# A down-projection weight loaded in another layout: twelve rows per partition and a rest of 256 rows over six or eight load engines

## The chip, the cores and the metric

The kernel runs on one core of one Trainium2 chip. The metric is the device time of one execution in microseconds (us). The time before is 231.94 us, the median of three runs (231.25 to 231.98). The core has TensorE (PE for matmuls, PEld for its weight loads), VectorE (DVE), ScalarE (ACT), GpSimd (POOL) and SyncE (SP), which here issues nearly all DMAs. A DMA is carried out by up to 16 DMA engines; they are called load engines here, to keep them apart from the compute engines. Each of them works through its own queue of packets, and when its part of a DMA is done it raises that DMA's semaphore.

## The reference, cut to what matters

One decode step for two sequences. The output is the sum of the input, a sliding-window attention and a gated unit, both fed by the same layer norm:

```python
xn = layernorm(A_x)                                  # (2, 1, 512)
# attention: 32 heads of 128 over 8 kv heads, the last 4096 of 32768 cached positions
q  = xn @ wq                                         # wq 512 x 4096
p  = softmax(q . k * 128**-0.5);  o = p . v          # k, v: 2 x 8 x 4096 x 128 read
# gated unit
h  = relu_gate(xn @ W_gate) * (xn @ W_up)            # W_gate, W_up 512 x 1792
out = x + o @ wo + h @ W_down                        # wo 4096 x 512, W_down 1792 x 512
```

All of it is float32. Keys and values of the window are 32 MB each, wq and wo 8 MB each, the three weights of the gated unit 3.5 MB each: some 95 MB, every byte read once.

## The kernel before, in words

**Loads.** Every large tile lies in a ring of four buffers (`ring`, `RING = 4`, L17 and L60) of up to 32 KB per partition. SP issues the loads in this order: two halves of wq, W_gate, W_up, then keys and values in tiles of 4 MB in turn (`load_kv`, L108), then `load_down` (L92, called at L445), then wo in two tiles, the first in one piece, the second in four pieces of 8, 5, 2 and 1 rows per partition (L475 to L480). A load into the ring waits until the tile that had the buffer has been used. All these loads stand in the load engines' queues in the order in which SP issues them. An ordinary load covers all 128 partitions, and each of 16 load engines gets eight of them.

**The rest of W_down before.** W_down has 1792 rows of 2 KB. `load_down` cuts them into 32 runs of 56 rows. Of each run 48 rows go into the main DMA (L98: 12 rows for each of 128 partitions, 24 KB in one piece), and 8 rows are left over, as four pieces of two rows (4 KB). The left-over pieces, 256 rows or 512 KB, are loaded by five DMAs at L105: three that take 8 runs each (32 partitions, 128 KB) and two that take 4 runs each (16 partitions, 64 KB). The first four go into spare columns of the ring buffer; the last goes into the tile `wx` of its own (L90). A memset (L99) on POOL clears the partitions of a spare column that no DMA fills.

**The gated unit.** Matmuls at L240 make the gate and the up product, `g_ps` and `u_ps`. The 1792 columns are cut into four quarters of 448, one for each group of 32 partitions of the result; the four matmuls of a step work on different column groups of PE. ACT copies the gate (L245), DVE makes the relu (L247) and the product `hh` (L251, L255). Matmuls against the identity (L263, L268) turn `hh` so that the 1792 values lie along partitions as the rows of W_down do, and DVE copies them to `hT` (L273, L275). This is done while the first keys arrive. The down product itself (L469 to L473) is made near the end.

**Attention.** For each group of heads, keys are transposed on PE (L296, result `pk`), copied to `kT` in a pool of two buffers (`ktp`, L61) by DVE and ACT in turn (L285), multiplied with q (L309, result `s`), put through a softmax (L315 on) and multiplied with the values (L373, result `o`). The order of all instructions is written out by hand.

**The end.** After the last values come the down product (`project` with `dw` and `wx`), the spreading of the last heads (L403) and the product with wo (L460, result `y_ps`), row by row of the wo tiles as their pieces land. One DVE copy (L482) and one DMA (L483) bring the result out.

Of the kernel before, what the change touches and what calls it, by code (L numbers as in the profile page):

```python
# [9 lines left out]
F32 = mybir.dt.float32  # L10
AF = mybir.ActivationFunctionType
ALU = mybir.AluOpType
# [8 lines left out]
def kernel(  # L21
# [12 lines left out]
    nc = tc.nc  # L34
    P = 128
    B, _, D = x.shape
# [3 lines left out]
    F = w_gate.shape[1]  # L40
    W = min(4096, max(256, SK // 4))
    KC = D // P
# [3 lines left out]
    Q = 4  # L46
# [6 lines left out]
    PK = P // 2  # L53
    J = W // PK
    FB = F // P
    FQ = F // Q
# [22 lines left out]
    def load_ff(w, name):  # L79
        return load(name, w.rearrange("(p k) f -> p k f", p=P), [P, KC, F])  # L80
# [3 lines left out]

    FR = F // 32
    FM = FB - 2
    assert FR == 4 * FM + 8
    wx = const.tile([16, 2, D], F32, name="wx")  # L90

    def load_down():  # L92
        t = ring.tile([P, FM + 4, D], F32, name="wd", tag="ring")
        runs = w_down.rearrange("(i x) e -> i x e", i=32)
        main = bass.AP(
            tensor=w_down.tensor, offset=w_down.offset, ap=[[FR * D, 32], [FM * D, 4], [1, FM * D]]
        )
        nc.sync.dma_start(t[:, 0:FM].rearrange("p k e -> p (k e)"), main)  # L98
        nc.gpsimd.memset(t[32:64, FM + 2:], 0.0)  # L99
        for i, n, dst in (  # L100
            (0, 8, t[0:32, FM:FM + 2]), (8, 8, t[32:64, FM:FM + 2]), (16, 8, t[0:32, FM + 2:]),
            (24, 4, t[32:48, FM + 2:]), (28, 4, wx),
        ):
            src = runs[i:i + n, 4 * FM:, :].rearrange("i (y s) e -> i y (s e)", s=2)
            nc.sync.dma_start(dst.rearrange("p s e -> p (s e)"), src)  # L105
# [25 lines left out]
    ident = const.tile([P, P], F32, name="ident")  # L131
# [7 lines left out]
    eps_t = const.tile([32, 1], F32, name="eps_t")  # L139
    nc.vector.memset(eps_t, EPS)  # L140

    hT = const.tile([P, FM + 6, B, 16], F32, name="hT")
# [66 lines left out]
    for kc in range(KC):  # L209
        for r in range(R):  # L210
            for c in range(C):
                n = r * C + c
                nc.tensor.matmul(  # L213
                    q_ps[r][32 * c:32 * c + 32, :], xnT[:, 0, kc, :], wqt[kc // 2][:, kc % 2, n * 512:(n + 1) * 512],
                    start=(kc == 0), stop=(kc == KC - 1),
                )
    gw = load_ff(w_gate, "wg")
    uw = load_ff(w_up, "wu")
    for r in range(R):
        qs = work.tile([P, 512], F32, name=f"qs{r}", tag="qs")  # L220
# [6 lines left out]
        for b in range(B):  # L227
            dst = qz[:, r * B + b].rearrange("p (a s h k) -> p a s h k", a=NP, s=S1, h=2)
# [3 lines left out]
                )  # L232


    g_ps = ps_kt.tile([P, FQ], F32, name="g_ps", tag="kt")
    u_ps = ps_kt.tile([P, FQ], F32, name="u_ps", tag="kt")
    for dst, wt in ((g_ps, gw), (u_ps, uw)):
        for kc in range(KC):
            for c in range(Q):
                nc.tensor.matmul(  # L240
                    dst[32 * c:32 * c + 32, :], xnT[:, 1, kc, :], wt[:, kc, c * FQ:(c + 1) * FQ],
                    start=(kc == 0), stop=(kc == KC - 1),
                )
    gs = work.tile([P, FQ], F32, name="gs", tag="qs")
    nc.scalar.copy(gs, g_ps)  # L245
    gr = work.tile([P, FQ], F32, name="gr", tag="qs")
    nc.vector.scalar_tensor_tensor(gr, gs, 0.0, gs, op0=ALU.is_gt, op1=ALU.mult)  # L247
    hh = work.tile([P, FB, 32], F32, name="hh", tag="qs")
    gv = gr.rearrange("p (i x) -> p i x", i=8)
    uv = u_ps.rearrange("p (i x) -> p i x", i=8)  # L250
    nc.vector.tensor_tensor(  # L251
        hh[:, 0:FM].rearrange("p k (i y) -> p i y k", i=8), gv[:, :, 0:4 * FM].rearrange("p i (y k) -> p i y k", y=4),
        uv[:, :, 0:4 * FM].rearrange("p i (y k) -> p i y k", y=4), op=ALU.mult,
    )
    nc.vector.tensor_tensor(  # L255
        hh[:, FM:].rearrange("p s (i y) -> p i y s", i=8),
        gv[:, :, 4 * FM:].rearrange("p i (y s) -> p i y s", s=2),
        uv[:, :, 4 * FM:].rearrange("p i (y s) -> p i y s", s=2), op=ALU.mult,
    )
    ht_ps = ps_1.tile([P, FM + 6, B], F32, name="ht_ps", tag="misc")  # L260
    for k in range(FM):
        for c in range(Q):
            nc.tensor.matmul(  # L263
                ht_ps[32 * c:32 * c + 32, k], hh[:, k], ident[:, 32 * c:32 * c + B], start=True, stop=True
            )
    for s in range(2):
        for c, p0, k, cols in ((0, 0, 0, (0, 32)), (1, 32, 0, (0, 32)), (2, 0, 2, (0, 32)), (3, 32, 2, (0, 16)), (3, 0, 4, (16, 32))):
            nc.tensor.matmul(  # L268
                ht_ps[p0:p0 + cols[1] - cols[0], FM + k + s], hh[:, FM + s, cols[0]:cols[1]],
                ident[:, 32 * c:32 * c + B], start=True, stop=True,  # L270
            )
    for n, lo, hi in ((P, 0, FM), (64, FM, FM + 2)):
        nc.vector.tensor_copy(hT[0:n, lo:hi, :, 0], ht_ps[0:n, lo:hi])  # L273
    for p0, n, lo, hi in ((0, 32, FM + 2, FM + 4), (32, 16, FM + 2, FM + 4), (0, 16, FM + 4, FM + 6)):
        nc.vector.tensor_copy(hT[p0:p0 + n, lo:hi, :, 0], ht_ps[p0:p0 + n, lo:hi])  # L275

# [117 lines left out]
    def finish(g):  # L394
        r, b = divmod(g, B)
        if b == 0:
            osb[r] = const.tile([HR, B, P], F32, name=f"osb{r}")
        nc.vector.tensor_scalar(osb[r][:, b], oa[g], rls[g], 2.0, op0=ALU.mult, op1=ALU.mult)

    def spread_heads(r):  # L400
        op = ps_1.tile([P, NJ, B], F32, name=f"op{r}", tag="misc")
        for e in range(NE):
            nc.tensor.matmul(  # L403
                op, spread[:, e].rearrange("h k e -> h (k e)"),
                osb[r][:, :, e * NJ:(e + 1) * NJ].rearrange("h b j -> h j b"),
                start=(e == 0), stop=(e == NE - 1),
            )
        nc.vector.tensor_copy(oT[:, r, :, :, 0], op)
# [33 lines left out]
    g = NG - 1  # L442
    scores(*pend.pop())
    vin = [load_kv(v_cache, "v", g, a) for a in range(NP)]
    dw = load_down()  # L445
    for _ in softmax(g):
        pass

# [9 lines left out]
    def project(lhsT, w, stop):  # L458
        for e in range(Q):
            nc.tensor.matmul(  # L460
                y_ps[32 * e:32 * e + 17, :], lhsT.rearrange("p b s -> p (b s)")[:, 0:17],
                w[:, e * P:(e + 1) * P], start=False, stop=stop,
            )
# [2 lines left out]
        values(g, a, vin[a])  # L466
        gather(g, a)
    finish(g)
    for k in range(FM + 4):  # L469
        n = P if k < FM else 64  # L470
        project(hT[0:n, k], dw[0:n, k], False)
    for k in range(2):
        project(hT[0:16, FM + 4 + k], wx[:, k], False)  # L473
# [38 lines left out]
```

## Time and profile before

| | |
|---|---|
| time, median of three runs | 231.94 us (231.25 to 231.98) |
| span of the profiled execution, first to last instruction | 230.3 us |
| PE busy | 184.4 us (80%) |
| DVE, ACT busy | 67.1 us, 48.4 us |
| bytes moved, mean rate | 95.15 MB, 413 GB/s |
| mean granted clock of TensorE | 0.933 |

The profile gives the span of its one execution and not that execution's time by the clock that timed the runs; the span is 1.6 us below the median. The page's first part is busy time by engine; a busy PE is not a PE at its peak, because matmuls are pipelined. Its second part cuts the span into 40 slices. "DMA" there, and "DMA share" in the windows, is the time that packets took as a share of 16 load engines; a packet is counted in the window in which it starts. The views do not keep the 16 load engines apart. The trace's semaphore records have the time at which each load engine finished its part of a DMA, without saying which engine it was.

### The profile page before, as it was taken

The numbers are of one execution on the slowest core, as the hardware profiler recorded it, in microseconds if no ns is written. First come the engines' busy times: TensorE is split into PE (matmuls) and PEld (weight loads), VectorE is DVE, ScalarE is ACT, GpSimd is POOL, SyncE is SP. The second block draws the span as 40 slices with busy tenths as digits, with TensorE's granted clock in tenths as the row PEclk, the third lists the DMA queues.
The fourth block names the chain that finished last, engine by engine and source line by source line (L and its number), as shares of the span: only waits on it lengthen the run. The fifth ranks groups of instructions, "written<-read, shape, count | busy, mean of one in ns | idle before, by whom it ended". The sixth has DMA issues, their size and how long they took to land.

```text
span 230.3 us, 4141 instructions
## 1 busy us (share of the span) xinstructions
PE 184.4 (80%) x1872; PEld 112.3 (49%) x1872; DVE 67.1 (29%) x136; ACT 48.4 (21%) x81; POOL 6.6 (3%) x23
## 2 busy tenths in 40 slices
PE   0295960849999889998999799589999974979593
PEld 0251220239666573664584565338566522148482
DVE  0500021023544462441472341147234123010000
ACT  2000100003444461540252331025133102000000
POOL 8100000000000000000000000000000100000000
PEclk9999799575999999999999999979999997699889
DMA  7999999999999999999999999999999999999980
GB/s 274 450 433 411 443 423 455 410 427 447 438 407 433 448 427 404 441 438 427 413 450 425 433 421 435 433 433 427 430 438 430 415 438 421 423 451 404 422 328 21
DMA packets 3936, 95.15 MB, mean 413 GB/s; under 512 B 454, under 2 KB 462, under 8 KB 848
## 3 DMA queue, kind: packets, MB, share of 16 engines
q1 hardware_dynamic: 3916, 94.90, 96.3%
q8 instruction: 14, 0.23, 0.4%
q14 instruction: 2, 0.02, 0.0%
q10 hardware_dynamic: 4, 0.00, 0.0%
HBM read 94.90 MB, written 0.00 MB: 412 GB/s over the span
## 4 chain that ended last, share of the span: by engine, by line
PE 46%; DMA 44%; DVE 4%; POOL 2%; ACT 1%; issue 1%; POOLq 0%
DMA k<-in_A_k_cache_dram 25%; PE pk L296 23%; DMA wd<-in_B_W_down_dram 11%; PE s L309 9%; DMA wo<-in_A_wo_dram 8%; PE o L373 5%; PE q_ps L213 3%; PE xt_ps L203 2%; PE pp L353 1%; DVE kT L285 1%; ACT p L342 1%; PE y_ps L460 1%; PE op L403 1%; PE oa L389 1%; POOL spread L155 1%
## 5 line engine op out<-in xcount | busy, mean ns | idle before, releaser
L296 PE MATMUL pk<-ident,k 128*128 128x128 f32 x512 | 68.1, 287 | 4.9 <-DMA k<-in_A_k_cache_dram 4.9
L296 PEld LDWEIGHTS pk<-ident,k 128*128 128x128 f32 x512 | 57.9, 146 | 19.8 <-issue 15.6
L285 DVE COPY kT<-pk 128x512 f32<-128x512 f32 x64 | 44.2, 691 | 50.6 <-PE pk L296 40.6
L285 ACT COPY kT<-pk 128x512 f32<-128x512 f32 x64 | 37.5, 586 | 81.8 <-PE pk L296 81.8
L309 PE MATMUL s<-kT,qz 128*32 128x512 f32 x256 | 31.9, 615 | 0.0
L373 PE MATMUL o<-v,pt 128*32 128x512 f32 x256 | 31.9, 631 | 0.0
L373 PEld LDWEIGHTS o<-v,pt 128*32 128x32 f32 x256 | 11.2, 116 | 15.3 <-issue 10.6
L309 PEld LDWEIGHTS s<-kT,qz 128*32 128x32 f32 x256 | 7.2, 112 | 12.8 <-issue 12.4
L213 PE MATMUL q_ps<-wq,xnT 128*32 128x512 f32 x64 | 10.9, 844 | 3.1 <-DMA wq<-in_A_wq_dram 2.6
L460 PE MATMUL y_ps<-wo,oT 128*17 128x128 f32 x256 | 9.3, 308 | 3.6 <-DMA wo<-in_A_wo_dram 3.6
L203 PE MATMUL xt_ps<-rep,xn 2*128 2x32 f32 x16 | 3.7, 400 | 10.2 <-DVE xn L197 10.2
L389 PE MATMUL oa<-on,pick 128*16 128x128 f32 x64 | 8.3, 273 | 4.1 <-DVE on L285 3.3
L285 DVE COPY on<-o 128x512 f32<-128x512 f32 x4 | 2.8, 692 | 29.9 <-PE o L373 29.9
L389 PEld LDWEIGHTS oa<-on,pick 128*16 128x16 f32 x64 | 5.8, 97 | 11.1 <-DVE on L285 7.0
L240 PE MATMUL u_ps<-wu,xnT 128*32 128x448 f32 x32 | 5.6, 870 | 6.8 <-DMA wu<-in_B_W_up_dram 6.8
L460 PEld LDWEIGHTS y_ps<-wo,oT 128*17 128x17 f32 x256 | 7.6, 111 | 5.1 <-DMA wo<-in_A_wo_dram 4.5
L203 PEld LDWEIGHTS xt_ps<-rep,xn 2*128 2x128 f32 x16 | 3.6, 319 | 10.2 <-issue 10.2
L285 ACT COPY on<-o 128x512 f32<-128x512 f32 x4 | 2.3, 586 | 26.6 <-PE o L373 26.6
L213 PEld LDWEIGHTS q_ps<-wq,xnT 128*32 128x32 f32 x64 | 2.5, 150 | 10.8 <-issue 6.6
L353 PE MATMUL pp<-ident,p 128*128 128x128 f32 x32 | 5.2, 295 | 2.4 <-ACT p L342 1.5
L342 ACT ACTIVATE p<-s,nm 128x1024 f32<-128x1024 f32 x4 | 4.5, 1116 | 12.5 <-DVE nm L337 12.5
L240 PEld LDWEIGHTS u_ps<-wu,xnT 128*32 128x32 f32 x32 | 1.4, 168 | 10.9 <-DMA wu<-in_B_W_up_dram 7.6
(77 smaller groups left out, 67.6 us busy)
## 6 DMA issues: line engine op xcount, KB each, us to landing
k<-in_A_k_cache_dram SPq DMA_DIRECT2D x8, 4096.0 KB, 26.5
v<-in_A_v_cache_dram SPq DMA_DIRECT2D x8, 4096.0 KB, 26.5
wq<-in_A_wq_dram SPq DMA_DIRECT2D x2, 4096.0 KB
wo<-in_A_wo_dram SPq DMA_DIRECT2D x1, 4096.0 KB, 28.3
wg<-in_B_W_gate_dram SPq DMA_DIRECT2D x1, 3584.0 KB, 29.7
wu<-in_B_W_up_dram SPq DMA_DIRECT2D x1, 3584.0 KB, 39.3
wd<-in_B_W_down_dram SPq DMA_DIRECT2D x1, 3072.0 KB, 26.4
wo<-in_A_wo_dram SPq DMA_DIRECT2D x1, 2048.0 KB, 20.6
```

What stands on the lines that cost most here:

```text
L155: nc.gpsimd.tensor_copy(spread[:, e, :, e], ident[0:HR, 0:HR])
L203: nc.tensor.matmul(xt_ps[:, o, kc, :], cols, rep.rearrange("r s b -> r (s b)"), start=True, stop=True)
L213: nc.tensor.matmul(q_ps[r][32 * c:32 * c + 32, :], xnT[:, 0, kc, :], wqt[kc // 2][:, kc % 2, n * 512:(n + 1) * 512], start=(kc == 0), stop ...
L240: nc.tensor.matmul(dst[32 * c:32 * c + 32, :], xnT[:, 1, kc, :], wt[:, kc, c * FQ:(c + 1) * FQ], start=(kc == 0), stop=(kc == KC - 1),)
L285: (nc.vector.tensor_copy if turn[0] % 2 else nc.scalar.copy)(dst, src)
L296: nc.tensor.transpose(pk[:, u * P:(u + 1) * P], kt_in[:, j * P:(j + 1) * P], ident)
L309: nc.tensor.matmul(ss[g][32 * q:32 * q + 32, :], qz[:, g, 32 * n:32 * n + 32], kt[:, h, q * 512:(q + 1) * 512], start=(a == 0 and s1 == 0 ...
L342: nc.scalar.activation(p, both, AF.Exp, bias=nm, scale=SCALE, accum_out=l)
L353: nc.tensor.transpose(pp[:, u], pv[:, lo:lo + P], ident)
L373: nc.tensor.matmul(o[32 * q:32 * q + 32, :], pts[g][:, jh, n].rearrange("p u k -> p (u k)"), v[:, lo:lo + 512], start=(s1 == 0 and jh == 0 ...
L389: nc.tensor.matmul(oa[g], pick[:, u, 8 - 8 * a:24 - 8 * a], ons[a][:, u], start=(a == 0 and u == 0), stop=(a == NP - 1 and u == 3),)
L460: nc.tensor.matmul(y_ps[32 * e:32 * e + 17, :], lhsT.rearrange("p b s -> p (b s)")[:, 0:17], w[:, e * P:(e + 1) * P], start=False, stop=stop,)
```

## The change

The main DMA of W_down now takes the first 1536 rows as they lie, 12 rows for each of 128 partitions. The last 256 rows go into a tile `wx` of their own in the pool `ktp`, with four DMAs: two of 120 rows each, whose source is six runs (`KX`) of four pieces of five rows (10 KB), and two of eight single rows (2 KB) each. POOL clears the first 64 partitions of `wx` before them. The order of the four pieces is such that each of the six runs covers four neighbouring partitions.

The gated unit follows that layout. The first 1536 columns go through `g_ps` and `u_ps` in quarters of 384 instead of 448. The last 256 columns have a product of their own, `x_ps` (32 partitions, gate and up in one bank), made by 8 more matmuls in the program, then a copy on ACT, a relu and four products on DVE into the cleared tile `hx`. Six matmuls turn `hx` for the down product, where there were ten. The down product has the same number of matmuls: 12 of 128 rows, five of 64 and one of 32, each in four parts, against 12 of 128, four of 64 and two of 16.

```diff
-    FR = F // 32
-    FM = FB - 2
-    wx = const.tile([16, 2, D], F32, name="wx")
+    FM = 12
+    KX = 6
+    LEFT = 2
+    FX = F - P * FM
+    RX = (FX - 8 * LEFT) // (8 * KX)
+    SX = RX + (LEFT > 0)
+    MQ = P * FM // Q
 
     def load_down():
-        t = ring.tile([P, FM + 4, D], F32, name="wd", tag="ring")
-        runs = w_down.rearrange("(i x) e -> i x e", i=32)
-        main = bass.AP(
-            tensor=w_down.tensor, offset=w_down.offset, ap=[[FR * D, 32], [FM * D, 4], [1, FM * D]]
-        )
-        nc.sync.dma_start(t[:, 0:FM].rearrange("p k e -> p (k e)"), main)
-        nc.gpsimd.memset(t[32:64, FM + 2:], 0.0)
-        for i, n, dst in (
-            (0, 8, t[0:32, FM:FM + 2]), (8, 8, t[32:64, FM:FM + 2]), (16, 8, t[0:32, FM + 2:]),
-            (24, 4, t[32:48, FM + 2:]), (28, 4, wx),
-        ):
-            src = runs[i:i + n, 4 * FM:, :].rearrange("i (y s) e -> i y (s e)", s=2)
-            nc.sync.dma_start(dst.rearrange("p s e -> p (s e)"), src)
-        return t
+        t = ring.tile([P, FM, D], F32, name="wd", tag="ring")
+        wx = ktp.tile([P, SX, D], F32, name="wx", tag="kT")
+        nc.gpsimd.memset(wx[0:64], 0.0)
+        nc.sync.dma_start(
+            t.rearrange("p k e -> p (k e)"), w_down[0:P * FM, :].rearrange("(p k) e -> p (k e)", p=P)
+        )
+        row = P * FM
+        for b in range(2):
+            src = bass.AP(
+                tensor=w_down.tensor, offset=w_down.offset + row * D,
+                ap=[[RX * D, KX], [KX * RX * D, 4], [1, RX * D]],
+            )
+            nc.sync.dma_start(wx[32 * b:32 * b + 4 * KX, 0:RX].rearrange("p k e -> p (k e)"), src)
+            row += 4 * KX * RX
+        for i in range(LEFT):
+            nc.sync.dma_start(wx[i:32:4, RX], w_down[row + 8 * i:row + 8 * i + 8, :])
+        return t, wx
...
+    hx = const.tile([32, SX, 64], F32, name="hx")
+    nc.gpsimd.memset(hx, 0.0)
...
+    x_ps = ps_1.tile([32, 2, FX], F32, name="x_ps", tag="o0")
+    for h, dst, wt in ((0, g_ps, gw), (1, u_ps, uw)):
         for kc in range(KC):
             for c in range(Q):
                 nc.tensor.matmul(
-                    dst[32 * c:32 * c + 32, :], xnT[:, 1, kc, :], wt[:, kc, c * FQ:(c + 1) * FQ],
+                    dst[32 * c:32 * c + 32, :], xnT[:, 1, kc, :], wt[:, kc, c * MQ:(c + 1) * MQ],
                     start=(kc == 0), stop=(kc == KC - 1),
                 )
+        for kc in range(KC):
+            nc.tensor.matmul(
+                x_ps[:, h], xnT[:, 1, kc, :], wt[:, kc, Q * MQ:], start=(kc == 0), stop=(kc == KC - 1)
+            )
...
+    gx = work.tile([32, 2, FX], F32, name="gx", tag="qs")
+    nc.scalar.copy(gx[:, 0], x_ps[:, 0])
+    nc.vector.scalar_tensor_tensor(gx[:, 1], gx[:, 0], 0.0, gx[:, 0], op0=ALU.is_gt, op1=ALU.mult)
+    for b in range(2):
...
+        nc.vector.tensor_tensor(
+            hx[:, 0:RX, 32 * b:32 * b + 4 * KX].rearrange("p s (e j) -> p e j s", j=4), g_in, u_in, op=ALU.mult
+        )
+    for i in range(LEFT):
+        lo = 2 * part + 8 * i
+        nc.vector.tensor_tensor(
+            hx[:, RX, i:32:4], gx[:, 1, lo:lo + 8], x_ps[:, 1, lo:lo + 8], op=ALU.mult
+        )
...
+    for k in range(SX):
+        m = 64 if k < RX else 32
+        nc.tensor.matmul(ht_ps[0:m, FM + k], hx[:, k, 0:m], ident[0:32, 0:B], start=True, stop=True)
```

More of the change, by code (lines that the diff above doesn't have):

```diff
@@ L55 @@
     FB = F // P
-    FQ = F // Q
     assert (B, REP, DH, S1, J) == (2, 4, P, 2, 64)
@@ L80, in load_ff @@
         return load(name, w.rearrange("(p k) f -> p k f", p=P), [P, KC, F])
[L87 to L106 removed]
+    FM = 12
[5 more added lines that the diff above has]
+    MQ = P * FM // Q
+    assert 8 * KX * RX + 8 * LEFT == FX
+    def load_down():
+        t = ring.tile([P, FM, D], F32, name="wd", tag="ring")
[3 more added lines that the diff above has]
+            t.rearrange("p k e -> p (k e)"), w_down[0:P * FM, :].rearrange("(p k) e -> p (k e)", p=P)
+        )
+        row = P * FM
[9 more added lines that the diff above has]
+        return t, wx
     def load_kv(cache, name, g, a):
@@ L140 @@
     nc.vector.memset(eps_t, EPS)
-    hT = const.tile([P, FM + 6, B, 16], F32, name="hT")
+    hT = const.tile([P, FM + SX, B, 16], F32, name="hT")
     nc.gpsimd.memset(hT, 0.0)
+    hx = const.tile([32, SX, 64], F32, name="hx")
+    nc.gpsimd.memset(hx, 0.0)
     oT = const.tile([P, R, NJ, B, 16], F32, name="oT")
@@ L232 @@
                 )
-    g_ps = ps_kt.tile([P, FQ], F32, name="g_ps", tag="kt")
-    u_ps = ps_kt.tile([P, FQ], F32, name="u_ps", tag="kt")
-    for dst, wt in ((g_ps, gw), (u_ps, uw)):
+    g_ps = ps_kt.tile([P, MQ], F32, name="g_ps", tag="kt")
+    u_ps = ps_kt.tile([P, MQ], F32, name="u_ps", tag="kt")
+    x_ps = ps_1.tile([32, 2, FX], F32, name="x_ps", tag="o0")
+    for h, dst, wt in ((0, g_ps, gw), (1, u_ps, uw)):
         for kc in range(KC):
@@ L240 @@
                 nc.tensor.matmul(
-                    dst[32 * c:32 * c + 32, :], xnT[:, 1, kc, :], wt[:, kc, c * FQ:(c + 1) * FQ],
+                    dst[32 * c:32 * c + 32, :], xnT[:, 1, kc, :], wt[:, kc, c * MQ:(c + 1) * MQ],
                     start=(kc == 0), stop=(kc == KC - 1),
                 )
-    gs = work.tile([P, FQ], F32, name="gs", tag="qs")
+        for kc in range(KC):
+            nc.tensor.matmul(
+                x_ps[:, h], xnT[:, 1, kc, :], wt[:, kc, Q * MQ:], start=(kc == 0), stop=(kc == KC - 1)
+            )
@@ L245 @@
+    gs = work.tile([P, MQ], F32, name="gs", tag="qs")
     nc.scalar.copy(gs, g_ps)
-    gr = work.tile([P, FQ], F32, name="gr", tag="qs")
+    gr = work.tile([P, MQ], F32, name="gr", tag="qs")
     nc.vector.scalar_tensor_tensor(gr, gs, 0.0, gs, op0=ALU.is_gt, op1=ALU.mult)
-    hh = work.tile([P, FB, 32], F32, name="hh", tag="qs")
-    gv = gr.rearrange("p (i x) -> p i x", i=8)
-    uv = u_ps.rearrange("p (i x) -> p i x", i=8)
+    hh = work.tile([P, FM, 32], F32, name="hh", tag="qs")
     nc.vector.tensor_tensor(
-        hh[:, 0:FM].rearrange("p k (i y) -> p i y k", i=8), gv[:, :, 0:4 * FM].rearrange("p i (y k) -> p i y k", y=4),
-        uv[:, :, 0:4 * FM].rearrange("p i (y k) -> p i y k", y=4), op=ALU.mult,
-    )
@@ L255 @@
[L255 to L258, printed above, removed]
-    )
-    ht_ps = ps_1.tile([P, FM + 6, B], F32, name="ht_ps", tag="misc")
+        hh.rearrange("p k y -> p y k"), gr.rearrange("p (y k) -> p y k", k=FM),
+        u_ps.rearrange("p (y k) -> p y k", k=FM), op=ALU.mult,
+    )
+    gx = work.tile([32, 2, FX], F32, name="gx", tag="qs")
@@ new lines @@
+    nc.scalar.copy(gx[:, 0], x_ps[:, 0])
+    nc.vector.scalar_tensor_tensor(gx[:, 1], gx[:, 0], 0.0, gx[:, 0], op0=ALU.is_gt, op1=ALU.mult)
+    part = 4 * KX * RX
+    for b in range(2):
+        g_in, u_in = (
+            a[:, b * part:(b + 1) * part].rearrange("p (j e s) -> p e j s", j=4, e=KX) for a in (gx[:, 1], x_ps[:, 1])
+        )
+        nc.vector.tensor_tensor(
+            hx[:, 0:RX, 32 * b:32 * b + 4 * KX].rearrange("p s (e j) -> p e j s", j=4), g_in, u_in, op=ALU.mult
+        )
@@ L261 @@
+    for i in range(LEFT):
[3 more added lines that the diff above has]
+        )
+    ht_ps = ps_1.tile([P, FM + SX, B], F32, name="ht_ps", tag="misc")
     for k in range(FM):
@@ L265 @@
             )
[L266 to L275, printed above, removed]
+    for k in range(SX):
+        m = 64 if k < RX else 32
+        nc.tensor.matmul(ht_ps[0:m, FM + k], hx[:, k, 0:m], ident[0:32, 0:B], start=True, stop=True)
+    nc.vector.tensor_copy(hT[:, 0:FM, :, 0], ht_ps[:, 0:FM])
+    nc.vector.tensor_copy(hT[0:64, FM:FM + RX, :, 0], ht_ps[0:64, FM:FM + RX])
+    if LEFT:
+        nc.vector.tensor_copy(hT[0:32, FM + RX, :, 0], ht_ps[0:32, FM + RX])
     HW = W // S1
@@ L444 @@
     vin = [load_kv(v_cache, "v", g, a) for a in range(NP)]
-    dw = load_down()
+    dw, wx = load_down()
     for _ in softmax(g):
@@ L468 @@
     finish(g)
[L469 to L473, printed above, removed]
+    for k in range(FM):
+        project(hT[:, k], dw[:, k], False)
+    for k in range(SX):
+        n = 64 if k < RX else 32
+        project(hT[0:n, FM + k], wx[0:n, k], False)
     spread_heads(R - 1)
```

## The prediction

> **What bounds the kernel now.** I read the page first, its DMA rows before its engine rows.
>
> ```profile
> span 230.3 us, 4141 instructions
> ...
> PE 184.4 (80%) x1872; PEld 112.3 (49%) x1872; DVE 67.1 (29%) x136; ACT 48.4 (21%) x81; POOL 6.6 (3%) x23
> ...
> DMA  7999999999999999999999999999999999999980
> DMA packets 3936, 95.15 MB, mean 413 GB/s; under 512 B 454, under 2 KB 462, under 8 KB 848
> q1 hardware_dynamic: 3916, 94.90, 96.3%
> q8 instruction: 14, 0.23, 0.4%
> ```
>
> The load engines are busy from the second slice to the 38th. q1, SP's queue, holds them for 96.3% of the span: 0.963 x 230.3 = 221.8 us of each of 16 engines on average. No faster compute moves the end; only fewer bytes, or a better share of them among the 16, can. q8 fetches TensorE's instructions: 0.4% x 16 x 230.3 = 14.7 us over 14 packets of 16 KB, 1.05 us each, on one load engine at a time. Next, how the last loads end, in windows of 1 us (the last two figures of a row are DMA share and GB/s), with one window of the steady part first:
>
> ```profile
> 80.00:100.00 20.00, 19.22 (x164) 12.35 (x164) 9.25 (x16) 8.40 (x14) 0.00 (x0) 1.00 1.01 432
> 220.00:221.00 1.00, 1.00 (x38) 0.96 (x32) 0.00 (x0) 0.00 (x0) 0.00 (x0) 0.86 0.94 391
> 221.00:222.00 1.00, 1.00 (x45) 1.00 (x40) 0.00 (x0) 0.00 (x0) 0.00 (x0) 1.00 0.91 379
> 222.00:223.00 1.00, 1.00 (x48) 1.00 (x41) 0.00 (x0) 0.00 (x0) 0.00 (x0) 1.00 0.79 320
> 223.00:224.00 1.00, 1.00 (x40) 0.75 (x28) 0.00 (x0) 0.00 (x0) 0.00 (x0) 1.00 0.64 254
> 224.00:225.00 1.00, 0.03 (x5) 0.00 (x1) 0.00 (x0) 0.00 (x0) 0.00 (x0) 1.00 0.35 139
> 225.00:226.00 1.00, 1.00 (x37) 1.00 (x40) 0.00 (x0) 0.00 (x0) 0.00 (x0) 1.00 0.14 55
> 226.00:227.00 1.00, 0.99 (x32) 0.47 (x25) 0.00 (x0) 0.00 (x0) 0.00 (x0) 1.00 0.03 10
> ```
>
> The engines don't end together. From 220 on they do 0.94 + 0.91 + 0.79 + 0.64 + 0.35 + 0.14 + 0.03 = 3.80 us on average, so evenly shared work would end at 223.8, while the last packets start after 226. Some 2.8 us is the most that sharing can bring. In 225 to 226 the share is 0.14 x 16 = 2.2 engines: two or three are late, the others done. The chain of waits says that the end hangs on these:
>
> ```profile
> 205.64 19.32 DMA wo<-in_A_wo_dram
> 225.00 1.88 PE y_ps L460 x56
> 226.88 0.46 PE y_ps L460 x8
> 227.37 0.29 DVE yo L482
> ```
>
> The four wo pieces land, PE does the last one's 8 matmuls in 0.46 us, and copy and store follow. After the last landing there are about 3.4 us to the span's end, none of which the change touches.
>
> Which engines are late the views don't say; the semaphore records let it be worked out. They give, for each DMA, the time at which each engine finished (us; my grouping):
>
> ```
> wd main  (16)    201.87 201.92 201.92 201.98 202.12 202.19 202.76 203.11 203.40 203.73 203.83 203.88 203.98 205.12 205.49 205.62
> third rest (8)   203.76 203.81 203.82 203.90 204.66 205.01 205.72 207.01
> wx         (4)   205.02 205.16 205.94 206.28
> last wo   (16)   221.68 221.74 223.34 223.39 223.41 223.43 223.56 224.51 | 224.60 224.74 225.05 225.19 225.50 225.86 226.59 226.84
> ```
>
> DMAs with eight runs outermost end in eight steps, those with four in four: the rest lies on eight engines, and four of them ("A") have all five DMAs, 80 KB each; four ("B") have three, 48 KB; eight ("C") have none. An engine's times chain: A ends wx at 205.02 to 206.28 and, 19.6 us later (two wo tiles at the pace below), the last wo at 224.60, 224.74, 225.50, 225.86. B ends the third rest at 203.81, 203.82, 205.72, 207.01, and the last wo at 223.39, 223.41, 226.84, 226.59 (the third took an instruction fetch on the way). So **both latest engines are in B**, though B carries less of W_down than A.
>
> **Why they are late.** A fetch delays its engine by its own 1.05 us and some more, together about 1.5 (the step by which a hit engine's finishing times fall behind the others'). Until wd main, eight engines had been hit by 11 fetches, three of them twice: two of B and six of C. In order the hits fall on C, C, B, B, C, C, C, C and again from the start. The only run of eight neighbouring numbers that holds two of 4 to 7 and six of 8 to 15 is 6 to 13, if A is 0 to 3, so the late pair would be engines 6 and 7. That is inferred: no record carries a number. Two of A have a smaller delay (0.7 to 1.0 us) from other fetches.
>
> The Trainium skill bears on the numbering ("DMA: Bandwidth & Descriptors", section on why a DMA increments its semaphore by 16): a DMA from SP uses the largest count up to 16 that divides the slowest dimension of both sides, and the lowest-numbered engines. The trace agrees as far as it shows counts (16, 8, 4). By that rule the new loads, 6 and 24 outermost, use engines 0 to 5, and those of eight rows 0 to 7.
>
> **The change, part by part.**
>
> *The rest on other engines.* The steady window gives 432 / 16 / 1.01 = 26.7 GB/s per engine: 80 KB cost 3.06 us, 48 KB 1.84, 4 KB 0.15. After: 0 to 5 get 2 x 4 x 10 KB + 4 KB = 84 KB, 6 and 7 get 4 KB. The last wo then ends so:
> - A: + 4 KB, +0.15: latest 225.86 -> 226.01.
> - B, engines 4 and 5: + 36 KB, +1.38: 223.41 -> 224.79.
> - B, engines 6 and 7: - 44 KB, -1.69: 226.84 -> 225.15, 226.59 -> 224.90.
> - C: unchanged, latest 225.19.
>
> The last is now 226.01 instead of 226.84: **-0.83 us**. An engine of A handles 10 packets for it (8 of 10 KB, 2 of 2 KB) where it handled 20 of 4 KB; what a packet costs beside its bytes the views don't show, and I take -0.05 for it, between 0 and the 0.15 above. What is late next is the A engine at 226.0, then C at 225.2; so the ends of this term are 0 (the pair isn't relieved) and -1.65 (A's small fetches absent), and, if the pair are 4 and 5, +1.38.
>
> *Issue.* SP issues five DMAs for W_down instead of six, but four wait for POOL, and POOL waits for a `kT` buffer.
>
> ```profile
> 179.08 1.92 PE L309 MATMUL s<-kT,qz 128*32 128x512 f32 x16
> 179.18 0.54 SPq L98 DMA_DIRECT2D wd<-in_B_W_down_dram  x1
> 179.26 0.94 POOL L99 MEMSET wd<- 32x1024 f32 x1 [172.89 <-PE pk L296]
> 179.77 2.98 SPq L105 DMA_DIRECT2D wd<-in_B_W_down_dram  x4
> 188.66 12.97 SPq L478 DMA_DIRECT2D wo<-in_A_wo_dram  x2
> 201.30 5.62 SPq L478 DMA_DIRECT2D wo<-in_A_wo_dram  x4
> L136 POOL MEMSET qz<- 128x1152 f32 x1 | 1.1, 1058 | 0.0
> ```
>
> The buffer that `wx` takes is read last by the scores at 179.08, done at 181.0. The memset has 3072 elements per partition against 1024 in 0.94 us and 1152 in 1.06: 2.8 us, to 183.8. Four issues at 2.98 / 4 = 0.75 us end at 186.8. Behind them on SP stands the first wo tile, now issued at 188.66. Nothing waits for the rest before the product at 208. The engines have work from wd main until 201.9, so even 10 us more would starve none: **0**. Uncovered, it costs its excess over some 201 us. The two lone 2 KB loads are in the 4 KB above.
>
> *The gated unit.* All this stands between the landing of W_up and the first keys.
>
> ```profile
> 41.41 5.57 PE L240 MATMUL u_ps<-wu,xnT 128*32 128x448 f32 x32 [6.75 <-DMA wu<-in_B_W_up_dram]
> L240 PE MATMUL g_ps<-wg,xnT 128*32 128x448 f32 x32 | 3.2, 541 | 1.1 <-DMA wg<-in_B_W_gate_dram 1.1
> 47.06 0.80 DVE L251 TENSOR_TENSOR hh<-gr,u_ps 128x384 f32<-128x384 f32 x1 [11.10 <-PE u_ps L240]
> 47.72 0.25 DVE L255 TENSOR_TENSOR hh<-gr,u_ps 128x64 f32<-128x64 f32 x1
> 47.92 0.95 PE L263 MATMUL ht_ps<-ident,hh 128*32 128x2 f32 x94 [0.93 <-DVE hh L251]
> L213 PE MATMUL q_ps<-wq,xnT 128*32 128x512 f32 x64 | 10.9, 844 | 3.1 <-DMA wq<-in_A_wq_dram 2.6
> k<-in_A_k_cache_dram SPq DMA_DIRECT2D x8, 4096.0 KB, 26.5
> 51.22 7.01 PE L296 MATMUL pk<-ident,k 128*128 128x128 f32 x38 [2.02 <-DMA k<-in_A_k_cache_dram]
> ```
>
> The 32 up matmuls run four at a time: 8 steps of 0.70 us. With 384 columns they take 4.77 us. The 256 columns apart have one column group, so their 8 steps of 0.70 x 256 / 448 = 0.40 add 3.2: the up product ends at 49.4, 2.4 later. Then come copy, relu and four small products, at 0.25 each from the row of 64 columns up to twice that, partly before 49.4: 1.0 to 2.5 us, and 12 short turns (0.95 us for 94, so 0.1). PE reaches the keys at 50.5 to 52.0; they end its wait at 51.22. So PE starts up to 0.8 us late. A key load lands 26.5 us after issue, and 4 MB at 432 GB/s take 9.7 of them; 16.8 us is queue. PE's lateness delays SP's next issue by as much and eats that: **0**, as long as it stays under some 10 us. The clear of `hx` on POOL (32 x 384, under 0.5 us) delays the first PE work, which goes on to wait 2.6 us for wq anyway: 0. Net 16 more PE instructions (8 program matmuls more, 4 fewer, each two matmuls and two weight loads) are 0.06 of the 3744 / 14 = 267 between two fetches: 14 stay 14.
>
> *The sum.* 230.3 - 0.83 - 0.05 = 229.4 for this execution; the median of the runs stands 1.64 above its span, so 231.94 - 0.88 = **231.1 us**.
>
> **Rivals.**
> 1. *The late pair are engines 4 and 5* (slower). 226.84 + 1.38 = 228.22: 233.3 us. It decides once the later of the two receives more than it loses. For it: no record numbers an engine, and the pair's place is an inference. Against: the hits would then skip 6 and 7.
> 2. *The load with six outermost doesn't use six engines.* The trace shows only 16, 8 and 4. On two engines, 240 KB each: 9.2 us instead of 3.06, so A's end goes to 226.0 + 6.1 and the time to 237.
> 3. *No change: what counts is the largest share of the rest.* It is 80 KB before and 84 after, and the Trainium skill's rules for kernel authors in the same page, on using all 16 engines, hold that a small outermost dimension confines a DMA to few. By this mechanism the end moves by +0.15, to 232.1. The records speak against it, since A, with 80 KB, ends 1 us before B; but if fetches fall on other engines in other executions (the runs span 0.7 us), the gain goes to about that: 231.6 to 232.1.
> 4. *A wait ahead of the wo loads starves the engines* (slower): the price is what the first wo issue passes 201 us. Worked out above it comes at 188.7, 12 us short.
>
> **How the numbers follow.** Forecast 0.60 (own range 230.3 to 231.5), rival 3 0.24, rival 1 0.08, rival 2 0.03, rival 4 and unforeseen slowing 0.05. A measurement here can tell about 0.3%, 0.7 us, from no change. The forecast's 0.88 lies just beyond that, so a tenth goes to "same": faster 0.54, same 0.31, slower 0.15. The range 230.2 to 232.6 holds the forecast and rival 3 and leaves out the slow cases.
>
> **What would show it.** In the windows of the last 6 us the DMA share should fall more steeply, with next to nothing after 225.7. The last wo should land 0.9 us sooner, and the gap between PE's wo groups shift by as much. The up product should end near 49.4 and PE start the keys by 52, with DMA share still 1.0 from 50 to 200. The first wo issue should stay before 195. It is wrong if the last landing is later than 226.8 (pair at 4 and 5), if a wd load is far longer than the others (two engines), or if the share dips near 190 to 205.

## The result, and the profile after

The changed kernel takes 233.11 us (median of 11 runs, 231.70 to 235.20) against 231.94 us before (11 runs, 231.25 to 232.13): a ratio of the means of 1.0043, 95% interval 1.0029 to 1.0057. That ratio leaves out the run of 235.20, which was in a slower state than the others. The change makes the kernel a little slower, where 231.1 us had been forecast. Its profiled execution has a span of 231.2 us, 0.9 more than before. The page after, its DMA rows:

```profile
span 231.2 us, 4161 instructions
...
DMA  7999999999999999999999999999999999999970
...
q1 hardware_dynamic: 3848, 94.90, 96.0%
q8 instruction: 14, 0.23, 0.4%
```

The load engines still fill the span, and there are still 14 instruction fetches in it. The windows of 1 us at the end of the changed kernel (the last two figures of a row are DMA share and GB/s), and its chain of waits:

```profile
222.00:223.00 1.00, 1.00 (x28) 0.81 (x23) 0.00 (x0) 0.00 (x0) 0.00 (x0) 0.50 0.73 297
223.00:224.00 1.00, 1.00 (x36) 0.91 (x32) 0.00 (x0) 0.00 (x0) 0.00 (x0) 0.78 0.69 270
224.00:225.00 1.00, 1.00 (x44) 0.99 (x40) 0.00 (x0) 0.00 (x0) 0.00 (x0) 1.00 0.36 141
225.00:226.00 1.00, 1.00 (x44) 0.82 (x40) 0.00 (x0) 0.00 (x0) 0.00 (x0) 1.00 0.09 37
226.00:227.00 1.00, 1.00 (x44) 0.97 (x40) 0.00 (x0) 0.00 (x0) 0.00 (x0) 1.00 0.07 27
227.00:228.00 1.00, 0.99 (x36) 0.48 (x24) 0.00 (x0) 0.00 (x0) 0.00 (x0) 1.00 0.02 6
```

```profile
186.95 31.03 DMA wo<-in_A_wo_dram
217.98 0.04 issue
218.02 9.83 PE y_ps L479 x248
...
227.86 0.46 PE y_ps L479 x8
```

The weight load for the last piece, in the timeline, with the wait ahead of it:

```profile
227.86 0.13 PEld L479 LDWEIGHTS y_ps<-wo,oT 128*17 128x17 f32 x8 [0.29 <-DMA wo<-in_A_wo_dram]
```

In 225 to 226 the share was 0.14 before and is 0.09 now: fewer engines are late. But 0.07 x 16 is about one engine in 226 to 227, and packets still start after 227. One engine alone is late, by more than the two were before. The first wo tile, 31.03 us on its way, lands late too, at 217.98, and PE works from there to the end almost without a pause. It still waits 0.29 us for the last piece, so the last landing sets the end here, but only just: with a little more work PE itself would have set it. The semaphore records (us, one figure for each engine that took part) narrow down which engine is late:

```
six-engine load (first)     203.46 203.50 203.80 204.14 204.60 206.53
single rows (first, 8)      202.26 203.92 205.19 205.27 205.55 205.87 206.33 208.27
last wo (the six latest)    224.95 225.00 225.12 225.43 225.90 227.81
```

One of the six engines 0 to 5 is two fetches behind as early as the first load of the rest (206.53, against 203.5 for those never fetched for). It keeps that delay, has 84 KB of the rest to do, and ends at 227.81. The engines that have only the single rows are 6 and 7, at 202.26 and 203.92: one never delayed, one once. (The numbers 0 to 7 go by the rule of the lowest-numbered engines on which the prediction built. The records show how many engines took part, and that the six are among the eight; they carry no numbers.)

What the prediction said of issue and compute, in the changed kernel's timeline:

```profile
181.00 2.66 POOL L98 MEMSET wx<- 64x3072 f32 x1 [174.28 <-PE s L328]
183.68 1.73 SPq L108 DMA_DIRECT2D wx<-in_B_W_down_dram  x2
185.46 1.39 SPq L111 DMA_DIRECT2D wx<-in_B_W_down_dram  x2
186.95 19.92 SPq L497 DMA_DIRECT2D wo<-in_A_wo_dram  x5
41.17 2.79 PE L249 MATMUL u_ps<-wu,xnT 128*32 128x384 f32 x32 [3.68 <-DMA wu<-in_B_W_up_dram]
43.77 1.67 PE L254 MATMUL x_ps<-wu,xnT 128*32 128x256 f32 x7
45.28 0.38 PE L254 MATMUL x_ps<-wu,xnT 128*32 128x256 f32 x1
47.22 0.89 PE L290 MATMUL ht_ps<-ident,hx 32*64 32x2 f32 x12 [0.76 <-DVE hx L274]
50.97 9.23 PE L315 MATMUL pk<-ident,k 128*128 128x128 f32 x57 [2.87 <-DMA k<-in_A_k_cache_dram]
45.00:200.00 155.00, 138.97 (x1244) 87.60 (x1245) 59.50 (x108) 45.36 (x77) 2.66 (x1) 0.94 1.00 430
```

The matmuls of the gated unit are done by 48.1, before the first keys. The first wo tile is issued at 186.95, earlier than before. The last row is a window over the whole stretch: DMA share 1.00. So neither compute nor issue holds up the load engines.

### The profile page after: what moved, and what is told of

It reads as the page before. It is cut to its first block, busy times and chain, and to the rows that moved or that the text cites. A ratio compares the mean times of both kernels' runs of the same rounds, so it can differ in the third digit from the quotient of the medians.

```text
span 231.2 us, 4161 instructions
## 1 busy us (share of the span) xinstructions
PE 186.1 (81%) x1880; PEld 115.4 (50%) x1880; DVE 67.6 (29%) x138; ACT 48.6 (21%) x82; POOL 8.7 (4%) x24
## 4 chain that ended last, share of the span: by engine, by line
PE 52%; DMA 38%; DVE 4%; POOL 3%; ACT 1%; issue 1%; POOLq 0%
DMA k<-in_A_k_cache_dram 24%; PE pk L315 23%; DMA wo<-in_A_wo_dram 13%; PE s L328 10%; PE o L392 6%; PE y_ps L479 4%; PE q_ps L221 2%; PE xt_ps L211 2%; PE oa L408 2%; PE pp L372 1%; DVE kT L304 1%; ACT p L361 1%; PE op L422 1%; DVE on L304 1%; POOL spread L163 0%
## 5 line engine op out<-in xcount | busy, mean ns | idle before, releaser
L479 PE MATMUL y_ps<-wo,oT 128*17 128x128 f32 x256 | 10.2, 332 | 3.3 <-DMA wo<-in_A_wo_dram 3.2
L221 PE MATMUL q_ps<-wq,xnT 128*32 128x512 f32 x64 | 9.2, 726 | 3.0 <-DMA wq<-in_A_wq_dram 2.4
L479 PEld LDWEIGHTS y_ps<-wo,oT 128*17 128x17 f32 x256 | 8.3, 120 | 5.1 <-DMA wo<-in_A_wo_dram 4.1
L98 POOL MEMSET wx<- 64x3072 f32 x1 | 2.7, 2656 | 174.3 <-PE s L328 174.3
L373 DVE TENSOR_TENSOR pt<-pp,own 128x512 f32<-128x512 f32 x8 | 5.5, 692 | 3.6 <-PE pp L372 3.6
```

The costliest lines, as they stand in the source:

```text
L98: nc.gpsimd.memset(wx[0:64], 0.0)
L221: nc.tensor.matmul(q_ps[r][32 * c:32 * c + 32, :], xnT[:, 0, kc, :], wqt[kc // 2][:, kc % 2, n * 512:(n + 1) * 512], start=(kc == 0), stop ...
L373: nc.vector.tensor_tensor(pts[g][:, jh].rearrange("p n u k -> p u n k"), pp.rearrange("p u (n k) -> p u n k", k=HK), own.rearrange("p h i ...
L479: nc.tensor.matmul(y_ps[32 * e:32 * e + 17, :], lhsT.rearrange("p b s -> p (b s)")[:, 0:17], w[:, e * P:(e + 1) * P], start=False, stop=stop,)
```

## The experiments

Theory E (load shares): the time is set by the load engine that ends last, and the change put 36 KB more on one that instruction fetches had already delayed twice. Rival C (compute): the split gated unit, the longer clear or the wait behind it costs the 0.4%. Times are compared with runs of the kernel before on the same chip: 231.87 us (29 runs) for the old shares, five and seven engines and the first version with thirteen rows; 231.99 (23) for all sixteen alike, the changed kernel again and the first attempt at more fetches; 232.10 (17) for "Engine 5 alone" and the second attempt; 231.93 (3) for the third. Times are medians, ratios are those of the means, with 95% intervals. "Steps" below are delays of some 1.5 us.

### The old shares in the new layout

```diff
+    REST = ((8, 0, 0), (8, 32, 0), (8, 0, 2), (4, 32, 2), (4, 0, 4))
-        for b in range(2):
+        for n, p0, k0 in REST:
             src = bass.AP(
                 tensor=w_down.tensor, offset=w_down.offset + row * D,
-                ap=[[RX * D, KX], [KX * RX * D, 4], [1, RX * D]],
+                ap=[[RX * D, n], [n * RX * D, 4], [1, RX * D]],
             )
...
```

The products into `hx` follow the same list.

> The changed kernel with the rest of W_down shared among the load engines as before (three loads over eight engines, two over four, pieces of two rows), everything else as changed. Theory E (load shares): the changed kernel is slower because the 36 KB that engines 4 and 5 took on lie on an engine that instruction fetches had already delayed twice; with the old shares the time is that of before within 0.2%, 231.9 us, the last wo load again 1.3 us or so behind the fifth latest engine. Rival C (compute): the split gated unit, the longer clear on POOL or the wait behind it costs the 0.4%; then this kernel stays at 233.0.

Measured: 232.05 us, ratio 1.0004 (0.9984 to 1.0023). All the new compute is in it (even one more small product), the clear on POOL too, and the loss is gone. Rival C falls; the 0.4% lies in the shares. The profile of this version does not repeat the end of before, though:

```profile
226.05 0.40 PE y_ps L471 x4
226.45 0.61 issue
227.06 0.41 PE y_ps L471 x4
```

Its last wo lands at 226.01 (226.84 before; 1.0 us behind the fifth latest engine, where some 1.3 was expected), and then PE stands still for 0.61 us in the middle of the last piece, so that its eight matmuls take 1.42 us where 0.46 is usual. The profile shows nothing that PE waits for there. A wait for instructions is possible (a fetch had begun at 224.6), but not shown. The changed kernel's profile has no such wait, so it is no part of the 0.4%.

### Five engines, and seven

```diff
-    KX = 6
+    KX = 5
```

> 240 rows over five load engines (two loads, five outermost, six rows a piece: 96 KB each) and 16 over eight. Tells whether the twice delayed engine of the six is number 5. Theory E with it at 5: it ends at 226.6 - 1.8 + 0.15 = 224.9 on the scale of the profile before, the latest of engines 0 to 3 at 225.86 + 0.76 = 226.6, and the time is about 231.7. Theory E with it at 4: 226.6 + 2.0 = 228.6, time 233.7. Its semaphore records then have five steps for the two loads, none or one of them two fetches late. Rival C: 233.0, as the compute is the same.

```diff
-    KX = 6
-    LEFT = 2
+    KX = 7
+    LEFT = 4
```

> 224 rows over seven load engines (seven outermost, four rows a piece: 64 KB each) and 32 over eight (8 KB each). Theory E: engines 0 to 3 end 0.3 us sooner than before at 225.6; the delayed one of 4 and 5 gets 72 KB instead of 48, 226.6 + 0.9 = 227.5; the delayed one of 6 and 7 gets 72 KB if it is number 6 (227.8) and 8 KB if it is number 7 (225.3). Time 232.6 to 232.9 either way; the steps of the seven-engine loads tell 6 from 7. Rival C: 233.0, not told apart by the time, by the steps alone.

Measured: five engines 232.18 us, 1.0021 (1.0008 to 1.0034); seven engines 233.32 us, 1.0067 (1.0049 to 1.0084). Their records:

```
five-engine load, first     204.10 204.10 204.39 205.01 205.32
  single rows, first (8)    202.50 204.03 204.08 | 206.14 206.15 206.44 207.04 207.38
seven-engine load, first    203.44 203.45 203.72 204.21 204.58 206.64 206.82
  single rows, first (8)    202.35 | 204.89 204.91 205.16 205.66 206.03 208.10 208.28
```

In the rows of single rows the bar sets apart the engines that carry nothing else of the rest (ahead of it) from those that carry the large loads too. With five, no engine of 0 to 4 is a whole step behind: 205.01 and 205.32 are two with a smaller delay, 0.9 and 1.2 us, which they have in wd main already (203.16 and 203.47, against 202.24 to 202.29 for the earliest and 203.80 to 203.95 for those one step late). Of 5, 6 and 7, ahead of the bar, two are one step behind and one is not. With seven, two of 0 to 6 are two steps behind, and engine 7, alone ahead of the bar, isn't delayed. Together, if the sets of engines lie in each other as the numbering says: **the delayed pair is 5 and 6; 7 is not fetched through**. Against their own runs of before, five engines lose 0.3 us where six lose 1.1, as 5 then carries 4 KB; they don't win, because 0 to 4 now carry 100 KB each. The forecasts of 231.7 and of 232.6 to 232.9 were some 0.5 us too low. With five, the last landing is 227.02 where 226.6 was forecast, on the engine that stood at 205.32; in the profile with seven, 5 and 6 had both been fetched for twice, and both got 72 KB. The end of the two in windows, five engines first:

```profile
226.00:227.00 1.00, 1.00 (x32) 0.48 (x24) 0.00 (x0) 0.00 (x0) 0.00 (x0) 1.00 0.04 16
227.00:228.00 1.00, 0.45 (x12) 0.13 (x8) 0.29 (x1) 0.00 (x0) 0.00 (x0) 1.00 0.06 16
```

```profile
226.00:227.00 1.00, 1.00 (x44) 0.81 (x36) 0.00 (x0) 0.00 (x0) 0.00 (x0) 1.00 0.12 49
227.00:228.00 1.00, 1.00 (x36) 0.54 (x24) 0.00 (x0) 0.00 (x0) 0.00 (x0) 1.00 0.05 20
```

With seven, 0.12 x 16 is two engines still at work in 226 to 227; with five it is 0.6. (The row after, with five, has 16 KB in 1 us: an instruction fetch, no load.)

### Thirteen rows for all, the rest over five engines

```diff
-    FM = 12
-    KX = 6
-    LEFT = 2
+    FM = 13
+    KX = 5
+    LEFT = 1
```

> 13 rows per partition in the main load (16 KB more on each of the 16 engines), 120 rows over five engines in pieces of three rows (48 KB each), eight over eight (2 KB). Theory E with the delayed engine at 5: engines 0 to 3 at 225.3, 5 at 225.4, 8 to 15 at 225.19 + 0.6 = 225.8, the last of all; 1.0 us sooner than before: 230.9. With it at 4: 227.3, time 232.4. Rival C: some 232.5 to 233, the part of the unit done apart is half as large.

Measured: 231.30 us, ratio 0.9975 (0.9964 to 0.9985): faster than before and than the change. All 12 executions lie within 0.4 us, 231.11 to 231.45. Its windows and its chain:

```profile
224.00:225.00 1.00, 0.98 (x36) 0.98 (x40) 0.00 (x0) 0.00 (x0) 0.00 (x0) 1.00 0.44 170
225.00:226.00 1.00, 0.98 (x32) 0.43 (x28) 0.00 (x0) 0.00 (x0) 0.00 (x0) 1.00 0.09 33
226.00:227.00 1.00, 0.36 (x8) 0.08 (x8) 0.29 (x1) 0.00 (x0) 0.00 (x0) 1.00 0.00 0
```

```profile
201.56 22.41 DMA wo<-in_A_wo_dram
224.02 1.90 PE y_ps L479 x56
225.95 0.46 PE y_ps L479 x8
```

More engines work until 225, none after 226. The last wo lands at 225.90 by the records, against 225.8 forecast. The time was forecast at 230.9 all the same, 0.4 too low: 0.1 of it is the landing, 0.2 what stands behind it (3.64 us to the span's end, 3.48 before). Engine 5 carries 18 KB here beyond the first twelve rows: 16 like every other, and 2 of the rest.

### All sixteen alike

```diff
-    FM = 12
+    FM = 14
```

with no rest, no `x_ps`, no `hx`.

> All 1792 rows of W_down in one load, 14 rows per partition, 32 KB more on each of the 16 engines; no rest, no product apart. Theory E (load shares): the engines 8 to 15 that were fetched for twice end at 225.19 + 1.22 = 226.4 on the scale of the profile before, 5 and 6 at 225.0 + 1.2 = 226.2, 0 to 3 at 222.8 + 1.2 = 224.0: time 231.5, a little under before and 0.2 us over the kernel with 13 rows. If an uneven share were worth nothing or the compute were the matter, it would be the fastest, under 231.0, as it has the fewest instructions.

Measured: 231.64 us, ratio 0.9988 (0.9979 to 0.9996), 11 executions within 231.54 to 231.78. It has the least work and the fewest instructions, and is 0.3 us behind the thirteen-row version; its last wo lands at 226.05 against 225.90. So an uneven share seems worth something, if it is laid on engines that have time. That is not clear of noise: the two were run on different chips, and the intervals of their ratios overlap. The Trainium skill ("DMA: Bandwidth & Descriptors", rules for kernel authors, on using all 16 engines) would have the rest on all of them; by these runs that beats the shares of before by 0.1% and the six engines by 0.5%, and a rest partly on engines 0 to 4 is at least as good.

### The changed kernel again

> The changed kernel itself, beside the others of this call. Theory E: two clusters of execution times, according to whether engine 5 is fetched for twice or once before its end: spans of 231.2 to 231.5 in most, 229.7 to 229.9 in about a quarter, median 233.0; a quarter, because two of the eight engines in the turn are fetched for once in 14 fetches and six twice. If the fetches always fell on the same engines, there would be one cluster.

Measured: 233.13 us, ratio 1.0040 (1.0017 to 1.0063). With the runs of the first result, 23 executions have spans in two clusters: 16 at 231.2 to 231.7, 7 (30%) at 229.7 to 229.9. Of 69 executions of the kernel before, 9 (13%) have spans of 229.2 to 229.5, and 60 lie at 229.9 to 230.6. Theory E gives one quarter for the changed kernel, where engine 5 alone decides, and one eighth for the kernel before, where both 5 and 6 must have been fetched for once: in its profile they follow each other in the turn, as third and fourth. The turn therefore starts at another engine in other executions. Two profiles of the changed kernel show it directly: in the first, engines 7 and 6 end the first single rows at 202.26 and 203.92, in this one at 202.29 and 205.3, so engine 6 had been fetched for once there and twice here. That the clusters come from this is inferred, as only slow-cluster executions of this kernel were profiled; what sets the start of the turn stays open.

### Engine 5 alone, once more

```diff
-    KX = 5
-    LEFT = 1
+    KX = 6
+    LEFT = 4
```

on the thirteen-row version.

> 13 rows per partition as in the faster version, but the rest over six engines (96 rows in pieces of two rows, 32 KB each) and 32 rows over eight (8 KB each), so that engine 5 gets 40 KB of the rest where it had 2. Theory E: engine 5, when fetched for twice, ends at 224.75 + 0.6 + 1.5 = 226.9 on the scale of the profile before, time 231.9 in about three quarters of the executions; else engines 8 to 15 at 225.8 set the end, and the time is 231.0 to 231.3, as with five engines. If it did not matter which engine carries the rest, it would be as the five-engine version in all executions, 231.3.

Measured: 232.26 us, ratio 1.0002 (0.9988 to 1.0016): the 0.6 us won by the thirteen-row version are gone, by 38 KB more on engine 5. The last wo lands at 227.18, the next latest engine at 225.88; 226.9 had been forecast. Spans: 10 of 12 at 230.3 to 230.7, two at 229.2, as low as the best with five engines. Two are fewer than a quarter; with 12 executions that is no contradiction.

### More fetches: three attempts

All three add tiny matmuls, whose results nothing uses, to the kernel before. The first:

```diff
+    idle_ps = ps_1.tile([32, 2], F32, name="idle_ps", tag="o0")
+    def idle(n):
+        for _ in range(n):
+            nc.tensor.matmul(idle_ps, ident[:, 0:32], ident[:, 0:2], start=True, stop=True)
+    idle(256)      # before the gate product, and again before the up product
```

> The kernel before with 512 tiny program matmuls (2048 PE instructions) that nothing uses, half before and half after the gate product, where PE waits for W_gate and W_up: about eight more instruction fetches, one for each of the eight engines that take them in turn. Theory E: each of them, 5 and 6 among them, ends 1.5 us later; 226.84 becomes 228.3 and the time 233.4, with no more than some us of delay for PE at the first keys and DMA share still 1.0. If fetches are not what makes engines late, the extra instructions are hidden and the time stays at 231.9.

The second does this on four column groups in turn, 160 + 160 + 96 + 96 times.

> The kernel before with 512 tiny program matmuls (2048 PE instructions) that nothing uses, now on four column groups in turn, 160 before the gate product, 160 before the up product and 96 after each of the first two key tiles: about eight more instruction fetches, one for each engine of the turn, without the 34 us that PE lost in the first attempt. Theory E (fetches make the late engines): each of the eight ends 1.5 us later, 226.84 becomes 228.3, time 233.4, with DMA share 0.97 or more from 60 to 200. If fetches are not what makes engines late: 231.9. If PE is again late by over 10 us the share dips and the run says nothing.

The third puts 8 ahead of every step of the key transposes. There are 128 such steps, not 64 as its expectation says, so it added 4096 PE instructions.

> The kernel before with 8 tiny program matmuls (32 PE instructions) ahead of each of the 64 key steps, overwritten by the transposes that follow: 2048 more PE instructions, about eight more fetches, spread evenly over 50 to 190 us so that PE is not held up by them. Read from the records of wd main: with 11 fetches before it, five engines were one step (1.5 us) late and three two steps. Theory E: with about 19, five are two steps late and three are three steps, and the last wo lands 1.5 us later on engine 5 or 6, at 228.3 or so; the DMA share stays at 0.97 or more. If fetches don't make the steps, the pattern stays 5 and 3. The time itself may be longer, as PE has some 8 us more work and little slack.

Measured: 266.58 us (1.149), 249.47 us (1.072) and 272.48 us (1.176). As tests of the time they say nothing: PE was held up and the loads ran out of work. In the first the matmuls of one column group took 51 us of PE, in the second PE stood for 42.9 us while its instructions came in, block by block, in the third its extra work was more than it had room for. The first's group of tiny matmuls and one of its windows; the second's wait ahead of them (us, times) and one of its windows; one window of the third:

```profile
L239 PE MATMUL idle_ps<-ident 128*32 128x2 f32 x1024 | 51.3, 189 | 0.7 <-issue 0.7
...
80.00:90.00 10.00, 10.00 (x153) 8.06 (x155) 0.00 (x0) 0.00 (x0) 0.00 (x0) 0.50 0.01 2
```

```profile
its engine sat idle before it (us, times) until:
  issue: 42.9, 21
...
108.00:110.00 2.00, 2.00 (x18) 1.73 (x19) 1.65 (x3) 0.83 (x2) 0.00 (x0) 1.00 0.00 0
```

```profile
100.00:150.00 50.00, 48.34 (x910) 31.62 (x909) 17.13 (x30) 13.96 (x24) 0.00 (x0) 1.00 0.83 346
```

But running dry lets all engines catch up, and then the records count fetches from zero. In the second the loads stood still from 106 to 112 us. Of the fetches after that, the first came at 119.7, and the key load that landed next had one engine 1.3 us behind the other fifteen; after the second, at 133.1, there were two. By wd main seven had come (119.7 to 216.2), and its engines ended at 218.20 to 218.49 (eight), 219.15 (one), 219.77 to 220.12 (seven). Seven fetches, seven engines one step late, none two. The one at 219.15 fell behind after 146.4, where another queue (q14) fetched 8 KB of instructions; the kernel before has two such fetches, and two engines with a smaller delay. The first attempt repeats the count: its loads stood almost still from 126 to 130 us, seven fetches followed up to wd main (136.8 to 234.3), and the engines ended at 236.26 to 236.72 (eight), 237.39 (one) and 237.90 to 238.23 (seven). In the third the engines ended the 8-row wo load together, at 250.44 to 250.93; one fetch came at 254.1; the last wo landed at 255.45 to 255.92 on fifteen engines and at 257.27 on one. One fetch, one engine, 1.35 us later than the next latest. In the kernel before, 11 fetches had made five engines one step late and three two: 5 + 2 x 3 = 11. That was not the test that was planned, but it shows that fetches make the steps.

## Why the prediction was wrong

**What bounds the kernel: right.** DMA share, the last landing, 3.4 us behind it (231.2 - 227.81 in the changed kernel). That nothing of those 3.4 us would change held there, but not in every version: with the old shares they became 4.45, by the slow last piece on PE.

**"The late pair would be engines 6 and 7": wrong, and the whole miss.** They are 5 and 6, so one of the pair got 36 KB more instead of 44 KB less. The step took eight neighbouring numbers as the only set with two of 4 to 7 and six of 8 to 15; the fetches skip 7. The records of before could not tell, since its rest loads end in eights and fours; a load over five engines and one over seven could.

**The shares: right engine by engine.** For 4 KB more the latest of engines 0 to 3 was put at 226.01; 225.90 was measured. For 36 KB more on a twice delayed engine the rule gives 226.59 + 1.38 = 227.97; 227.81 was measured. The sum of -0.83 became 227.81 - 226.84 = +0.97 because the right price stood at the wrong engine.

**Rival 1 came true by half.** One of the pair was in 0 to 5, not both. Its price of 233.3 holds: 233.11. It was given 0.08; an inference on which the sign hangs, and which no record of the trace could check, deserved far less trust. The range stopped at 232.6 for the same reason.

**Rival 2 (not six engines): no.** The records have six steps, and five and seven in the experiments; on the count the Trainium skill's rule holds in each. **Rival 3 (the largest share counts): no**; shares of 80 KB before and 84 after differ by 4 KB, and the time by 1.2 us. **Rival 4 (starved loads): no**; DMA share 1.01 from 186 to 210 us, and the first wo issue at 186.95 where 186.8 was worked out.

**Issue and the gated unit: the zeros hold, one size was off.** The clear took 2.66 us (2.8). The up product ended at 45.7, not 49.4. The 49.4 had been worked out from rows of an execution in which the granted clock was 0.67 in 41 to 51 us; here it was 0.92 (before first):

```profile
41.00:51.00 10.00, 6.85 (x148) 2.58 (x148) 1.53 (x7) 0.00 (x0) 0.00 (x0) 0.67 1.02 439
```

```profile
41.00:51.00 10.00, 6.21 (x149) 3.69 (x149) 2.17 (x9) 0.36 (x1) 0.00 (x0) 0.92 1.03 441
```

Over the up product alone the granted clock was 0.57 before (41 to 47 us) and 1.00 here (41 to 46). The prediction took a row's duration without asking what clock it had been measured at. PE reached the keys 2.9 us early, and nothing changed.

**What was to be seen.** A steeper fall was forecast, with next to nothing after 225.7; the fall is a little steeper from 225 on and then has a tail of one engine, to after 227. "Wrong if the last landing is later than 226.8 (pair at 4 and 5)" names the sign that came, but not the engine.

**The spread over executions** was seen as a possible cause of rival 3 alone. It is a property of both kernels: in the changed one a quarter or so of the executions lie 1.5 us lower. The sum took from one profile which engine is hit how often.

## What to carry to other kernels

Where the load engines are full to the end, the time is set by the one that ends last, and TensorE's instruction fetches, at about 1.5 us each, can decide which that is; a rest of some hundred KB is best laid on engines that are seen to have time, and evenly where that isn't known (here the even share was 0.1% better than before, and half a per cent better than the six engines). Loads over five, six and seven engines, compared in the semaphore records, tell which engines are late, as far as the rule for the numbers holds, so an inference from a count of eights and fours need not carry the sign of a forecast. Look at the times of many executions for clusters: a layout that wins in one state of the fetch turn can lose in most.

## What the runs showed that was not expected

- Instruction fetches go through eight load engines in turn, 5, 6 and six of 8 to 15, and not 7; a fetch of 1.02 us put its engine 1.35 us behind the next latest in the cleanest case.
- The turn differs between executions of one program: ahead of the rest of W_down, engine 6 had been fetched for once in one profile of the changed kernel, and twice in another. With it go two clusters of spans: 7 of 23 of the changed kernel are 1.5 us lower than the others, 9 of 69 before are 0.8 lower.
- In the second attempt, with a DMA share of 1.01 from 33 to 54 us, PE got a block of instructions only every 6 to 7 us (fetches at 33.7, 40.3, 46.4, 53.4). The 2048 added instructions brought 8 more fetches, so a block is some 256 instructions; tiny matmuls that used them up faster stood for 42.9 us in all. It is no fixed pace: in the third attempt two fetches are 3.5 us apart (83.9 and 87.4).
- Tiny matmuls on one column group cost PE 51 us for 1024 in the first attempt, 50 ns each, with a granted clock of 0.50 in 40 to 60 and 70 to 90 us; on four column groups in turn, 94 took 0.95 us in the kernel before (granted clock 0.83 in 47 to 51). Part of the difference is the clock.
